# Gating two token tiles at once in an attention, MoE and FFN kernel on one Trainium2 core

## Chip, cores and metric

The kernel runs on one core of one Trainium2 chip. Its time is device microseconds of one execution; the median of a few executions is compared. The core's engines are TensorE (PE), VectorE (DVE), ScalarE (ACT), GpSimd (POOL) and SyncE (SP), which issues most of the DMAs. Each works through its own instructions in order and waits on semaphores for the others.

## What is computed

Three layers, each feeding the next, in float32; the token count N is 4 x 576 = 2304:

```python
# attention: 4 batches, 8 heads, 576 positions, 64 wide; window 128, ALiBi bias
scores = scale * np.matmul(q, k.transpose(0, 1, 3, 2))
mask = (rel >= 0) & (rel < window)
scores = np.where(mask, scores + bias[None], -1000000000.0)
attn = np.exp(scores - np.max(scores, axis=-1, keepdims=True))
attn = attn / (np.sum(attn, axis=-1, keepdims=True) + 1e-09)
x = np.matmul(attn, v)                                  # then (N, 512)
# mixture of 8 experts, 512 -> 1024 -> 512, two per token
noisy_logits = x @ w_gate + np.log1p(np.exp(x @ w_noise)) * noise
top2 = np.argpartition(-noisy_logits, 2, axis=1)[:, :2]  # weights: softmax over the two
out[mask] += top2_w[mask, k, None] * (np.maximum(x[mask] @ w1[e], 0.0) @ w2[e])
# FFN 512 -> 2048 -> 512
h = out @ w_in
r = np.maximum(h, 0.0)
result = (r * r) @ w_out
```

## The kernel before

The 2304 tokens are 18 tiles of 128. Attention takes a tile in two halves of four heads each, so there are 36 steps v. The order of the instructions is the order in which the Python code issues them; there is no scheduler. The loop over v (near the end of the function) does in each pass: `s_step(v + 2)`, `t_step(v + 1)`, `pv_step(v)` and the norm of v, so three steps are in work at once. Between these stand slots: `at(v, slot, f, ...)` files a piece of other work under a step and a slot, and `run(v, slot)` issues it. Slots 0 to 3 come after each head's score operation within `s_step`, slot 4 after the transposes, slot 5 after the norm.

- `s_step`: 16 QK matmuls (L245) into a `psb` bank; per head one VectorE operation (L255) that adds the bias, writes `p` and accumulates the row's extreme into `mx`; then the exponentials on ScalarE (L262). A row of scores spans 192 keys. Where a batch begins, part of them lies before the batch: `parts(i)` then cuts the 128 rows into two halves with different first columns, GpSimd writes 0 to the masked part (L251), and VectorE and ScalarE work on each half by itself (two instructions a head instead of one). These are the tiles 0, 4, 5, 9, 13 and 14, so 12 steps.
- `t_step`: six transposes of `p` on TensorE (L273) into `psa`, and two copies to `pt` on ScalarE (L275).
- `pv_step`: PV (L297) into the other `psb` bank; the norm on VectorE: L308 (the first reader), L311, L314, which writes half of the rows `xi`. After the second half SP sends `xi` to DRAM (L320).

The gate of tile i runs in the slots of the steps after v = 2i + 1. `gate_t` transposes `xi` on TensorE (L327) and copies it to `xt` on ScalarE (L329). `gate_m` multiplies with the gate weights (L335), then exponential and logarithm on ScalarE (L339, L340). `gate_o` finds the top two on VectorE (L345 to L357; L355 writes the one-hot `oh`). `rank` counts, with a triangular matrix, which row of its expert each token gets (L365), and adds `oh` to the running counts `acc` (L366). `place` works out the position in the table of slots on VectorE (L373 to L396), and GpSimd scatters the token numbers into it with two indirect DMAs (L400), a small memset of `spacer` (L399) ahead of each.

The gate's TensorE results share one PSUM bank, `psc`; `psa` has three and `psb` two (`bank`, L69). In every fourth step GpSimd also prepares a block of expert weights: a cast (L114) and a subtraction (L116) of 128 x 1024 elements. At the end of the attention SP reads the first expert's part of the table (L466), GpSimd gathers its rows (L413, three indirect DMAs), `x_in` transposes them (L420), and the first expert's matmuls begin (L437). The rest of the kernel, the experts (L437, L687) and the FFN (L794, L827), isn't touched.

Of the kernel before, what the change touches and what calls it, by code (L numbers as in the profile page):

```python
# [46 lines left out]
def attn_moe_ffn(ctx: ExitStack, tc: tile.TileContext, qt, kt, vt, wgn, noise, w1, w2, w_in, w_out,  # L47
# [180 lines left out]
    def s_step(v, now):  # L228
# [94 lines left out]
    def gate_t(i):  # L323
# [4 lines left out]
        G["xt", i] = wk.tile([128, 4, 128], F32, name="xt", tag="xt", bufs=2)  # L328
        nc.scalar.activation(out=G["xt", i], in_=ps, func=AF.Copy)  # L329

    def gate_m(i):
        gp = bank("c")
        xt = G.pop(("xt", i))
        for c in range(4):
            nc.tensor.matmul(gp[:, 0:16], xt[:, c, :], wg_sb[:, c, :], start=(c == 0), stop=(c == 3))  # L335
        gs = wk.tile([128, 8, 8], F32, name="gs", tag="gs", bufs=3)
        G["gs", i] = gs
        G["gp", i] = gp
        nc.scalar.activation(out=gs[:, 0], in_=gp[:, 8:16], func=AF.Exp)  # L339
        nc.scalar.activation(out=gs[:, 1], in_=gs[:, 0], func=AF.Ln, bias=1.0)  # L340

    def gate_o(i, n):
        gs = G["gs", i]
        if n == 0:
            nc.vector.tensor_tensor(out=gs[:, 2], in0=gs[:, 1], in1=nz_sb[:, i, :], op=OP.mult)  # L345
        elif n == 1:
            nc.vector.tensor_tensor(out=gs[:, 2], in0=gs[:, 2], in1=G.pop(("gp", i))[:, 0:8], op=OP.add)
        elif n == 2:
            nc.vector.max(out=gs[:, 3], in_=gs[:, 2])
        elif n == 3:  # L350
            nc.vector.max_index(out=sel[:, i, :], in_max=gs[:, 3], in_values=gs[:, 2])
        elif n == 4:
            oh = wk.tile([128, 2, 8], BF16, name="oh", tag="oh", bufs=3)
            G["oh", i] = oh
            nc.vector.tensor_tensor(out=oh, in0=iota8[:, None, :].to_broadcast([128, 2, 8]),  # L355
                                    in1=sel[:, i, 0:2, None].to_broadcast([128, 2, 8]), op=OP.is_equal)
            nc.vector.tensor_tensor(out=gap[:, i:i + 1], in0=gs[:, 3, 1:2], in1=gs[:, 3, 0:1], op=OP.subtract)  # L357

    def rank(i):
        oh = G["oh", i]  # L360
        rk = bank("c")
        G["rk", i] = rk
        for m, (l, r) in enumerate(((tri, oh), (ones, acc))):
            for k in range(2):
                nc.tensor.matmul(rk[:, 0:8], l, r[:, k, :], start=(m + k == 0), stop=(m + k == 2))  # L365
        nc.vector.tensor_tensor(out=acc, in0=acc, in1=oh, op=OP.add)  # L366

    def place(i, n):
        gs, oh = G["gs", i], G["oh", i]
        t, pf = gs[:, 4], gs[:, 5, 0:2]  # L370
        if n == 0:
            G["ri", i] = wk.tile([128, 2, 8], I32, name="ri", tag="ri", bufs=2)
            nc.vector.tensor_copy(G["ri", i][:, 0], G.pop(("rk", i))[:, 0:8])  # L373
            return
        ri = G["ri", i]
        if n == 1:
            nc.vector.tensor_scalar(ri[:, 1], ri[:, 0], 7, None, op0=OP.logical_shift_right)
            nc.vector.scalar_tensor_tensor(out=t, in0=ri[:, 0], scalar=float(E * NJ), in1=base8, op0=OP.mult,
                                           op1=OP.add)
            if i == EARLY:  # L380
                nc.vector.tensor_copy(snap[:, 0, 0:1], ri[0:1, 0, 0:1])
            if i == FIRST:
# [504 lines left out]
```

## Time and profile before

| | us |
|---|---|
| three executions | 1077.39, 1080.24, 1073.08; median 1077.39 |
| the profiled execution | 1080.85, of which span 1079.1 |
| busy TensorE, VectorE, ScalarE, GpSimd | 1033.2, 531.6, 419.0, 190.6 |
| mean granted TensorE clock | 0.964 of full |

Times in the profile are microseconds. The granted clock is the share of full speed that TensorE is given; it has two levels, 1.2 and 2.4 GHz, so that a mean between 0.5 and 1 says how long it stood at each. A row of a timeline is the start, the length and a run of alike instructions; in brackets stands the idle time of that engine just before it, and which instruction's end released it.

### The profile page before, as it was taken

To read this page: it belongs to the slowest core of one execution; us is meant where nothing else is said; L and a number is where in the kernel's file an instruction comes from. 1 tells how busy PE (TensorE), PEld (TensorE's weight loads), DVE (VectorE), ACT (ScalarE), POOL (GpSimd) and SP (SyncE) were. 2 spreads that over 40 slices of the span, in tenths; PEclk is the share of its full clock that TensorE was granted. 3 is DMA by queue.
4 is the path that set the end of the run, shared out by engine and by line. 5 is a ranking of instruction groups with operands and counts; after the bars stand their busy time and mean duration, and the time that the engine had idled before them with its cause. 6 is when DMAs were issued, how large, how long until landed. Compare 5 with 4: busy or idle time off the path is not lost. (4 is left out here: it accounts for less than half of the span.)

```text
span 1079.1 us, 18812 instructions
## 1 busy us (share of the span) xinstructions
PE 1033.2 (96%) x7518; PEld 922.7 (86%) x7518; DVE 531.6 (49%) x1429; ACT 419.0 (39%) x799; POOL 190.6 (18%) x238
## 2 busy tenths in 40 slices
PE   7888887999999999999999999999999999999998
PEld 5666666988989898989898988998989989899897
DVE  4787774445757666675756234622414123141330
ACT  6766673333434334343433334522413223131321
POOL 2344442310302121121203000301001010000000
PEclk8898976899999999999999999999999999999999
DMA  8554441335564746464645326501011010100000
GB/s 305 198 183 160 163 148 51 104 103 176 181 219 157 221 155 219 167 224 146 225 166 196 108 71 215 177 21 49 30 40 33 27 50 20 49 21 20 11 11 20
DMA packets 53233, 130.53 MB, mean 121 GB/s; under 512 B 7168, under 2 KB 9488, under 8 KB 52752
## 3 DMA queue, kind: packets, MB, share of 16 engines
q1 hardware_dynamic: 45600, 108.22, 30.1%
q0 software_dynamic: 7536, 21.02, 6.2%
q8 instruction: 61, 1.00, 0.4%
q14 instruction: 36, 0.29, 0.1%
HBM read 99.81 MB, written 29.40 MB: 120 GB/s over the span
## 5 line engine op out<-in xcount | busy, mean ns | idle before, releaser
L794 PEld LDWEIGHTS psa<-xf,w 128*128 128x128 f32 x1728 | 207.1, 190 | 2.2 <-DVE xf L422 1.2
L794 PE MATMUL psa<-xf,w 128*128 128x256 f32 x1728 | 207.6, 282 | 1.0 <-DVE xf L422 1.0
L801 DVE TENSOR_TENSOR gt<-gr,psa 128x512 f32<-128x512 f32 x72 | 49.5, 687 | 215.1 <-ACT gr L800 214.9
L437 PE MATMUL psa<-xa,w 128*128 128x384 f32 x768 | 144.8, 338 | 0.0
L687 PE MATMUL psb<-w,ha 128*128 128x512 f32 x552 | 137.0, 397 | 0.0
L437 PEld LDWEIGHTS psa<-xa,w 128*128 128x128 f32 x768 | 133.2, 190 | 0.6
L116 DVE TENSOR_TENSOR w<-raw,w 128x1024 fp32r<-128x1024 f32 x68 | 83.8, 1232 | 80.4 <-ACT w L112 80.0
L687 PEld LDWEIGHTS psb<-w,ha 128*128 128x128 f32 x552 | 100.9, 188 | 20.1
L827 PE MATMUL psb<-w,g 128*128 128x512 f32 (+1 forms) x456 | 103.8, 380 | 0.0
L827 PE MATMUL psb<-wx,g 128*128 128x512 f32 (+1 forms) x456 | 103.5, 380 | 0.0
L437 PE MATMUL psa<-xb,w 128*128 128x256 f32 x768 | 100.9, 282 | 1.3 <-ACT xb L421 0.9
L437 PEld LDWEIGHTS psa<-xb,w 128*128 128x128 f32 x768 | 98.4, 189 | 1.6 <-ACT xb L421 1.0
L612 POOL DMA_INDIRECT yr<-yg,pos x36 | 35.7, 992 | 341.7 <-DVE yr L619 210.9
L827 PEld LDWEIGHTS psb<-wx,g 128*128 128x128 f32 x456 | 81.9, 188 | 15.4
L827 PEld LDWEIGHTS psb<-w,g 128*128 128x128 f32 x456 | 81.3, 188 | 15.1
L591 POOL TENSOR_TENSOR dcc<-dca,dcc 128x512 f32<-128x512 f32 x32 | 41.6, 1300 | 287.1 <-DVE dca L589 145.0
L687 PE MATMUL psb<-w,hb 128*128 128x512 f32 x384 | 92.1, 393 | 0.0
L112 ACT ACTIVATE w<-raw 128x1024 fp32r<-128x1024 f32 x68 | 71.9, 1057 | 41.8 <-DMA raw<-in_w_dram 26.9
L262 ACT ACTIVATE p<-p,mx 128x192 f32<-128x192 f32 (+3 forms) x192 | 75.5, 422 | 31.5 <-DVE mx L255 29.0
L800 ACT ACTIVATE gr<-psa 128x512 f32<-128x512 f32 x72 | 43.0, 598 | 114.9 <-PE psa L794 114.0
L687 PEld LDWEIGHTS psb<-w,hb 128*128 128x128 f32 x384 | 71.6, 188 | 15.3
L441 ACT ACTIVATE ha<-psa 128x384 fp32r<-128x384 f32 x64 | 31.5, 492 | 105.8 <-PE psa L437 102.2
(108 smaller groups left out, 1169.7 us busy)
## 6 DMA issues: line engine op xcount, KB each, us to landing
raw<-in_w_dram SPq DMA_DIRECT2D x64, 512.0 KB
v<-in_vt_dram SPq DMA_DIRECT2D x20, 520.0 KB
yg<-yo SPq DMA_DIRECT2D x40, 256.0 KB
bits<-in_w_in_dram SPq DMA_DIRECT2D x16, 512.0 KB
bits<-in_w_out_dram SPq DMA_DIRECT2D x16, 512.0 KB
xd<-xi SPq DMA_DIRECT2D x18, 256.0 KB
q<-in_qt_dram SPq DMA_DIRECT2D x17, 256.0 KB
out_dram<-yo SPq DMA_DIRECT2D x17, 256.0 KB
```

The lines of the kernel that those rows point to most:

```text
L112: nc.scalar.activation(out=c[:, 0, :], in_=r, func=AF.Copy)
L116: eng.tensor_tensor(out=c[:, 1, :], in0=r, in1=c[:, 0, :].bitcast(F32), op=OP.subtract)
L262: nc.scalar.activation(out=p2[j][p0:p1, a, c0:], in_=p2[j][p0:p1, a, c0:], func=AF.Exp, bias=mx[j][p0:p1, a:a + 1], scale=-1.0)
L437: nc.tensor.matmul(o, w[:, wp, f * 128:(f + 1) * 128], x[:, xp, d, :], start=(n == 0), stop=(n == 11))
L441: nc.scalar.activation(out=hi, in_=ps, func=AF.Relu)
L591: nc.gpsimd.tensor_tensor(out=cf, in0=af, in1=cf, op=OP.add)
L612: nc.gpsimd.indirect_dma_start(out=YR[i, k], out_offset=None, in_=yg, in_offset=bass.IndirectOffsetOnAxis(ap=pos[:, i, k:k + 1], axis=0))
L687: nc.tensor.matmul(py, h[:, hq], wc[:, wp, wsl], start=(f + n == 0), stop=(f == 7 and n == 2))
L794: nc.tensor.matmul(ph[:, f % 2, :], wc[:, wp, fs], xf[:, xp, d, 0:BLK], start=(n == 0), stop=(n == 11))
L800: nc.scalar.activation(out=gr, in_=ph, func=AF.Relu)
L801: nc.vector.tensor_tensor(out=gt, in0=gr, in1=ph, op=OP.mult)
L827: nc.tensor.matmul(py[:, c0:c1], g[:, f, gq, j * 128:(j + 1) * 128], wc[:, wp, w0 + c0:w0 + c1], start=(f + n == 0), stop=(f == 15 and n = ...
```

## The change

The gate works on pairs of tiles p, with v = 4p + 3 the pair's last step. The two transposes stay apart (steps 4p + 2 and 4p + 4, slot 4; `xt` gets four buffers), and the rest is issued once per pair: eight gate matmuls at step 4p + 5, slot 4; the VectorE operations on 2 x 8 columns at step 4p + 6, slots 0 to 2; the rank (12 matmuls, as the second tile of a pair also counts the first) at slot 5, behind PV; the positions at step 4p + 7, slots 0 to 3, with all four scatters at the last. Where a batch begins, the masked part is filled with 1e9 instead of 0, so that one exponential a head (scale -1) covers all 192 columns. The first expert's `x_in` and the readers of its first results move a slot or two.

```diff
-                    nc.gpsimd.memset(p2[j][p0:p1, :, 0:c0], 0.0)
+                    nc.gpsimd.memset(p2[j][p0:p1, :, 0:c0], 1.0e9)
...
-                for p0, p1, c0 in parts(i):
-                    nc.scalar.activation(out=p2[j][p0:p1, a, c0:], in_=p2[j][p0:p1, a, c0:], func=AF.Exp,
-                                         bias=mx[j][p0:p1, a:a + 1], scale=-1.0)
+                nc.scalar.activation(out=p2[j][:, a, :], in_=p2[j][:, a, :], func=AF.Exp, bias=mx[j][:, a:a + 1],
+                                     scale=-1.0)
...
+    def gate_m(p):
+        gp = bank("c")[:, 0:32].rearrange("p (q w) -> p q w", q=2)
+        for q in range(2):
+            xt = G.pop(("xt", 2 * p + q))
+            for c in range(4):
+                nc.tensor.matmul(gp[:, q, :], xt[:, c, :], wg_sb[:, c, :], start=(c == 0), stop=(c == 3))
...
+    def rank(p):
+        oh = G["oh", p]
+        rk = bank("c")[:, 0:16].rearrange("p (q w) -> p q w", q=2)
+        G["rk", p] = rk
+        for q in range(2):
+            terms = [(tri, oh[:, q])] + [(ones, oh[:, 0])] * q + [(ones, acc)]
+            for m, (l, r) in enumerate(terms):
+                for k in range(2):
+                    nc.tensor.matmul(rk[:, q, :], l, r[:, k, :], start=(m + k == 0),
+                                     stop=(m + k == len(terms)))
+        for q in range(2):
+            nc.vector.tensor_tensor(out=acc, in0=acc, in1=oh[:, q], op=OP.add)
...
+            for q in range(2):
+                for k in range(2):
+                    i = 2 * p + q
+                    nc.gpsimd.memset(spacer, 0.0)
+                    st = nc.gpsimd.indirect_dma_start(
...
-    for i in range(NT):
-        v = 2 * i + 1
-        at(v + 1, 4, gate_t, i)
-        at(v + 2, 0, gate_m, i)
-        for n, p in enumerate((3, 3, 4, 4, 5)):
-            at(v + 2, p, gate_o, i, n)
-        at(v + 3, 0, rank, i)
-        for n, p in enumerate((1, 2, 3, 4, 4, 5)):
-            at(v + 3, p, place, i, n)
+    last = NV - 1
+    for p in range(NT // 2):
+        v = 4 * p + 3
+        end = v == last
+        at(v - 1, 4, gate_t, 2 * p)
+        at(v + 1, 4, gate_t, 2 * p + 1)
+        at(v + 2, 0 if end else 4, gate_m, p)
+        o = v + 2 if end else v + 3
+        for n, c in enumerate((0, 0, 0, 1, 2)):
+            at(o, c, gate_o, p, n)
+        at(o, 5, rank, p)
+        for n, c in enumerate((0, 1, 1, 2, 2, 3)):
+            at(o + 1, c, place, p, n)
...
-    for j, p in enumerate(((-1, 4), (0, 0), (0, 4))):
+    for j, p in enumerate(((-1, 5), (0, 4), (0, 5))):
...
-    at(last + 2, 5, out_a, 0, 0)
+    at(last + 3, 4, out_a, 0, 0)
     at(last + 3, 4, mm1_a, 0, 2)
     at(last + 3, 5, out_a, 0, 1)
-    at(last + 4, 0, out_a, 0, 2)
+    at(last + 3, 5, out_a, 0, 2)
```

On TensorE, before, the steps around one tile's gate read like this (L365 rank, L327 gate transposes, L335 gate matmuls; L273, L297 and L245 are transposes, PV and QK):

```order
L365 LDWEIGHTS tri [waits DVE_49]
L365 MATMUL psc<-oh,tri 128x8 [waits Activation_49]
...
L365 LDWEIGHTS ones
...
L273 MATMUL psa<-cst,p_1887 128x128 [waits Activation_49] x2
...
L327 MATMUL psc<-cst,xi 128x128 [waits DVE_49]
L327 MATMUL psc<-cst,xi 128x128 x3
L297 MATMUL psb<-v,pt 64x65 [waits PE_49]
...
L245 MATMUL psb<-k,q 64x192 [waits DVE_49,PE_49]
...
L335 MATMUL psc<-wg_sb,xt 128x16 [waits Activation_49]
L335 MATMUL psc<-wg_sb,xt 128x16 x3
L273 MATMUL psa<-cst,p_1961 128x128 x3
...
L297 MATMUL psb<-v,pt 64x65 [waits DVE_49,PE_49]
```

After, the same engine from the gate matmuls of a pair (L336) to its rank (L371); L272, L296 and L245 are transposes, PV and QK, and L326 the gate transposes of the next pair's first tile:

```order
L336 MATMUL psc<-wg_sb,xt 128x16 [waits Activation_49]
L336 MATMUL psc<-wg_sb,xt 128x16 x7
L296 MATMUL psb<-v,pt 64x65 [waits DVE_49,PE_49]
...
L245 MATMUL psb<-k,q 64x192 [waits DMAHW2_49,DVE_49,PE_49]
...
L272 MATMUL psa<-cst,p_1756 128x128 [waits Activation_49] x2
...
L326 MATMUL psc<-cst,xi 128x128 [waits DVE_49,Activation_49]
L326 MATMUL psc<-cst,xi 128x128 x3
L296 MATMUL psb<-v,pt 64x65 [waits PE_49]
...
L371 LDWEIGHTS tri [waits DVE_49]
L371 MATMUL psc<-oh,tri 128x8 [waits Activation_49]
...
L371 LDWEIGHTS ones
```

The gate matmuls have moved from before the transposes of a step to behind them, and the rank from the head of a step to its end, behind the next pair's gate transposes and PV; it waits for VectorE and for ScalarE, as before.

On GpSimd, before, in a stretch of plain steps (L114 and L116 weights, L400 scatters):

```order
L114 CAST w_1726<-raw 128x1024 [waits DMAHW5_49,Pool_49]
L116 TENSOR_TENSOR w_1726<-raw,w_1726 128x1024 [waits Pool_49]
L399 MEMSET spacer 1x1
L400 DMA slots<-tok,pos 9728x1 [waits DMASW0_49,DVE_49]
L399 MEMSET spacer 1x1 [waits Pool_49]
L400 DMA slots<-tok,pos 9728x1 [waits DMASW1_49]
L399 MEMSET spacer 1x1 [waits Pool_49]
L400 DMA slots<-tok,pos 9728x1 [waits DMASW2_49,DVE_49]
```

After, at a burst that stands ahead of a batch's beginning (L413 scatters, L251 memset of the masked part):

```order
L412 MEMSET spacer 1x1
L413 DMA slots<-tok,pos 9728x1 [waits DMASW0_49,DVE_49]
L412 MEMSET spacer 1x1 [waits Pool_49]
L413 DMA slots<-tok,pos 9728x1
...
L413 DMA slots<-tok,pos 9728x1
L251 MEMSET p_780 64x2x64 [waits PE_49,Activation_49]
L251 MEMSET p_786 64x2x64 [waits PE_49,Activation_49]
...
L114 CAST w_987<-raw 128x1024 [waits DMAHW6_49]
L116 TENSOR_TENSOR w_987<-raw,w_987 128x1024 [waits Pool_49]
```

The scatters have moved together in fours, and the memset and the weight preparation of the steps that follow stand behind all four.

## Rows read from the trace of the kernel before

**Rows 1.** The page: the granted TensorE clock in 40 slices of 27 us.
```profile
PEclk8898976899999999999999999999999999999999
```

**Rows 2.** Windows of four steps: length, busy us (count) by engine, TensorE clock, DMA, GB/s.
```profile
48.40:67.84 19.44, 15.97 (x237) 12.67 (x232) 16.33 (x99) 16.04 (x42) 7.88 (x12) 0.90 0.49 165
67.84:86.37 18.53, 15.42 (x252) 11.77 (x248) 13.22 (x83) 10.57 (x31) 8.33 (x13) 0.91 0.51 179
...
148.01:169.16 21.15, 18.10 (x244) 14.58 (x239) 13.28 (x83) 12.30 (x34) 7.59 (x10) 0.74 0.35 114
169.16:195.82 26.66, 19.19 (x231) 16.35 (x223) 13.10 (x83) 9.12 (x23) 7.20 (x11) 0.63 0.20 60
```

**Rows 3.** Timeline of TensorE over one tile: start, us, instructions, idle before and releaser.
```profile
28.03 0.20 PE L365 MATMUL psc<-oh,tri 128*128 128x8 bf16 x2 [0.39 <-DVE oh L355]
...
28.14 0.85 PE L273 MATMUL psa<-cst,p 128*128 128x128 f32 x6
28.90 0.66 PE L327 MATMUL psc<-cst,xi 128*128 128x128 f32 x4
29.48 1.13 PE L297 MATMUL psb<-v,pt 128*64 128x65 f32 x32
30.43 0.83 PE L245 MATMUL psb<-k,q 64*64 64x192 f32 x16
31.33 1.06 PE L335 MATMUL psc<-wg_sb,xt 128*128 128x16 f32 x8
32.24 0.85 PE L273 MATMUL psa<-cst,p 128*128 128x128 f32 x6
```

**Rows 4.** Timeline of all engines at one weight preparation, 74.8 to 78.6 us.
```profile
74.89 1.04 POOL L114 CAST w<-raw 128x1024 fp32r<-128x1024 f32 x1
...
76.02 2.33 POOL L116 TENSOR_TENSOR w<-raw,w 128x1024 fp32r<-128x1024 f32 x1
...
76.46 1.93 DVE L355 TENSOR_TENSOR oh<-iota,sel 128x16 bf16<-128x16 uint32 x1
...
78.44 0.21 PE L365 MATMUL psc<-oh,tri 128*128 128x8 bf16 x2 [2.20 <-DVE oh L355]
```

**Rows 5.** Groups by line and shape, first 260 us: busy us, mean ns; idle before.
```profile
L355 DVE TENSOR_TENSOR oh<-iota,sel 128x16 bf16<-128x16 uint32 x18 | 11.2, 621 | 0.0
...
L366 DVE TENSOR_TENSOR acc<-acc,oh 128x16 bf16<-128x16 bf16 x18 | 6.0, 331 | 1.0 <-PE psc L365 0.8
```

**Rows 6.** Timeline of all engines in the tile of rows 3.
```profile
29.94 0.85 ACT L275 ACTIVATE pt<-psa 128x384 f32<-128x384 f32 x2
...
30.68 0.60 ACT L329 ACTIVATE xt<-psc 128x512 f32<-128x512 f32 x1
...
33.35 0.17 DVE L349 MAX8 gs<-gs 128x8 f32<-128x8 f32 x1
```

**Rows 7.** Timeline at two scatters (66 us) and at the early gathers (180 us).
```profile
66.09 0.99 POOL L400 DMA_INDIRECT slots<-tok,pos  x1 [0.22 <-issue]
...
67.84 0.16 DVE L308 TENSOR_SCALAR rs<-psb 128x4 f32<-128x4 f32 x1 [1.09 <-PE psb L297]
...
179.79 0.95 POOL L413 DMA_INDIRECT xr<-xd,gidx  x1 [0.30 <-issue]
...
181.94 0.16 DVE L308 TENSOR_SCALAR rs<-psb 128x4 f32<-128x4 f32 x1 [5.48 <-remote]
...
183.05 1.52 PE L273 MATMUL psa<-cst,p 128*128 128x128 f32 x6
```

**Rows 8.** The view of rows 5: exponentials, and the memset of the masked part.
```profile
L262 ACT ACTIVATE p<-p,mx 128x192 f32<-128x192 f32 x96 | 37.3, 445 | 19.0 <-DVE mx L255 19.0
...
L262 ACT ACTIVATE p<-p,mx 64x192 f32<-64x192 f32 x32 | 14.4, 451 | 5.2 <-DVE mx L255 4.3
...
L262 ACT ACTIVATE p<-p,mx 64x64 f32<-64x64 f32 x32 | 11.0, 345 | 6.1 <-DVE mx L255 5.3
...
L251 POOL MEMSET p<- 64x256 f32 x16 | 4.5, 319 | 0.2
```

More of the change, by code (lines that the diff above doesn't have):

```diff
@@ L327, in gate_t @@
             nc.tensor.transpose(ps[:, c, :], xi[:, c * 128:(c + 1) * 128], ident)
-        G["xt", i] = wk.tile([128, 4, 128], F32, name="xt", tag="xt", bufs=2)
+        G["xt", i] = wk.tile([128, 4, 128], F32, name="xt", tag="xt", bufs=4)
         nc.scalar.activation(out=G["xt", i], in_=ps, func=AF.Copy)
[L331 to L339, printed above, removed]
+    def gate_m(p):
[4 more added lines that the diff above has]
+                nc.tensor.matmul(gp[:, q, :], xt[:, c, :], wg_sb[:, c, :], start=(c == 0), stop=(c == 3))
+        gs = wk.tile([128, 8, 2, 8], F32, name="gs", tag="gs", bufs=2)
+        G["gs", p] = gs
+        G["gp", p] = gp
+        nc.scalar.activation(out=gs[:, 0], in_=gp[:, :, 8:16], func=AF.Exp)
@@ L340, in gate_m, with gate_o @@
         nc.scalar.activation(out=gs[:, 1], in_=gs[:, 0], func=AF.Ln, bias=1.0)
-    def gate_o(i, n):
-        gs = G["gs", i]
+    def gate_o(p, n):
+        gs = G["gs", p]
+        two = slice(2 * p, 2 * p + 2)
         if n == 0:
-            nc.vector.tensor_tensor(out=gs[:, 2], in0=gs[:, 1], in1=nz_sb[:, i, :], op=OP.mult)
+            nc.vector.tensor_tensor(out=gs[:, 2], in0=gs[:, 1], in1=nz_sb[:, two, :], op=OP.mult)
         elif n == 1:
-            nc.vector.tensor_tensor(out=gs[:, 2], in0=gs[:, 2], in1=G.pop(("gp", i))[:, 0:8], op=OP.add)
+            nc.vector.tensor_tensor(out=gs[:, 2], in0=gs[:, 2], in1=G.pop(("gp", p))[:, :, 0:8], op=OP.add)
@@ L354, in gate_o @@
[L354 to L366, printed above, removed]
@@ L368, in place @@
-    def place(i, n):
-        gs, oh = G["gs", i], G["oh", i]
-        t, pf = gs[:, 4], gs[:, 5, 0:2]
+            oh = wk.tile([128, 2, 2, 8], BF16, name="oh", tag="oh", bufs=2)
+            G["oh", p] = oh
+            nc.vector.tensor_tensor(out=oh, in0=iota8[:, None, None, :].to_broadcast([128, 2, 2, 8]),
+                                    in1=sel[:, two, 0:2, None].to_broadcast([128, 2, 2, 8]), op=OP.is_equal)
+            nc.vector.tensor_tensor(out=gap[:, two, None], in0=gs[:, 3, :, 1:2], in1=gs[:, 3, :, 0:1], op=OP.subtract)
@@ new lines, in rank @@
+    def rank(p):
[8 more added lines that the diff above has]
+                                     stop=(m + k == len(terms)))
+        for q in range(2):
+            nc.vector.tensor_tensor(out=acc, in0=acc, in1=oh[:, q], op=OP.add)
@@ L371, in place @@
+    def place(p, n):
+        gs, oh = G["gs", p], G["oh", p]
+        t, pf = gs[:, 4], gs[:, 5, :, 0:2]
         if n == 0:
-            G["ri", i] = wk.tile([128, 2, 8], I32, name="ri", tag="ri", bufs=2)
-            nc.vector.tensor_copy(G["ri", i][:, 0], G.pop(("rk", i))[:, 0:8])
+            G["ri", p] = wk.tile([128, 2, 2, 8], I32, name="ri", tag="ri", bufs=2)
+            nc.vector.tensor_copy(G["ri", p][:, 0], G.pop(("rk", p)))
             return
-        ri = G["ri", i]
+        ri = G["ri", p]
@@ L504, in attn_moe_ffn @@
     load_to(1)
-    for v in range(-2, NV + 4):
+    for v in range(-2, NV + 3):
         s_step(v + 2, v)
```

47 lines of the change are left out of this document (23 added, 24 removed).

## The prediction

> **What bounds the kernel now.** I read the page's slices first [rows 1]: the granted clock is below full in the first seven of 40 slices, some 190 us, which hold the attention with the gate. What follows is a matmul stream that the change doesn't touch, so only the first 200 us can move. Second I cut that stretch into windows of four half-tile steps, two token tiles each [rows 2]. The reader is to see that no engine is full: in 67.84 to 86.37 TensorE works 15.4 of 18.5 us, VectorE 13.2, ScalarE 10.6; in a window where a batch begins (48.40 to 67.84) VectorE and ScalarE come to 16. The stretch is a chain of hand-overs, and its last window, 26.66 us at a clock of 0.63, is the worst. Third, TensorE's timeline over a tile without trouble [rows 3]. From start to start: rank 0.11 us, transposes 0.76, gate transposes 0.58, PV 0.95, QK 0.90, gate matmuls 0.91. Four steps are 4 x (0.76 + 0.95 + 0.90) = 10.4 plus 2 x (0.11 + 0.58 + 0.91) = 3.2, so 13.6 us of work against 18.5. Two waits that the gate makes are in the same rows: 0.39 for `oh`, 0.41 for `xt`.
>
> **The change part by part.** The sum is made against the profiled execution's own 1080.85 us, which is 3.5 above the median of the runs shown (1077.39); the forecast is put on the median at the end.
>
> 1. *The collision.* VectorE's `oh` takes 1.93 us at 76.46, and ends within 0.05 us of GpSimd's weight subtraction (76.02 + 2.33); TensorE's rank waits 2.20 behind it [rows 4]. By line, L355 takes 621 ns on average over 18 and L366 331 ns, where a gate operation of this size takes 0.17 us alone [rows 5, 6]: 18 x (0.621 - 0.17) + 18 x (0.331 - 0.17) = 8.1 + 2.9 = 11 us, nearly all on TensorE's path. GpSimd works in order and runs ahead, so after the change its cast and subtraction, 3.5 us from 74.89 to 78.35, follow the burst of scatters of step 4p+3 (4.8 us, part 4), 8.3 us from that step's slot 3; the pair's gate operations come at step 4p+6, some 9 us after it by my schedule below. I take them as clear of each other, and the collision as gone: 1.9 us in a clean window. The margin is thin; without it rival 3 holds.
> The Trainium skill ("SBUF — State Buffer", Who interferes with whom) says that a VectorE operation with two SBUF inputs contends with a GpSimd instruction that reads SBUF, and that the loser is blocked for the whole of it. The trace agrees with that, by the 1.93 us above. By this rule the change only moves what is exposed, for most of the gate's operations have two SBUF inputs; that is rival 3 again, and with it the sum would come to about nothing.
>
> 2. *A new wait at the rank.* There is one `psc` bank. In step 4p+6 the rank comes behind PV, and between the gate matmuls and it lie the gate transposes of the next pair, so it starts only when ScalarE has copied those to `xt`. ScalarE, in order, comes to `xt` behind the step's exponentials and two `pt` copies [rows 6]. In the tile of before `xt` ended at 30.68 + 0.60 = 31.28, and PV's work at 30.43, where QK starts [rows 3]: 0.85 us late. To that comes VectorE: seven instructions of the pair's gate stand ahead of the step's first score operations, 0.17 us each [rows 6] and some 0.20 apart, which makes the exponentials, and so `xt`, 1.4 us later: 2.2 us. Bounds: 0 (ScalarE ahead) to 3.1 (one more `pt` copy in between); I take 2.2, which both rows give. Behind the waiting rank stand QK and the transposes, so all of TensorE stands.
>
> 3. *What goes with the pairing.* The waits of 0.39 and 0.41, twice a pair, go (1.6 us). Rank has 12 matmuls for two tiles, 0.33 us against 0.22. VectorE has some ten gate operations of 0.2 us fewer a pair, 2 us, hidden while VectorE works 13.2 of 18.5 us; were it the bound, they would be worth these 2 us. The gate matmuls are the same 1.8 us, in one place. By hand a pair is 13.7 of work, 2.2 at the rank and 1.1 for two QKs that wait for a last score operation: 17.0. The clock: after the long wait that ends at 181.94 six transposes take 1.52 us instead of 0.85 [rows 7, 3], and of a clean window I put 18.5 - 13.6 - 1.9 - 1.4 (small waits) = 1.6 down to it. Half of that, 0.8, I leave in, since a wait of 2 us remains: 17.8 against 18.5, so **-1.5** for the two clean windows. In 148.01 to 169.16, where the clock is 0.74 and the window 2.6 longer, I let two thirds of that stay and take the same 0.7: **-1.6**.
>
> 4. *One exponential a head where a batch begins.* A head costs 451 + 345 ns there against 445 for a whole one [rows 8]: 4 x 0.35 = 1.4 us less of ScalarE a step, 12 steps, worth something only where ScalarE ends last (16.04 of 19.44 us in the second window). Against it, the exponential now reads the masked part and so waits for GpSimd's memsets, 0.32 us each [rows 8], which stand behind four scatters of 0.99 with 0.22 between [rows 7]: 4.8 us. These begin at slot 3 of step 4p+7, the next step's exponentials about 3.0 later: a wait of 4.8 + 0.6 - 3.0 = 2.4, less the 1.4 saved, +1.0 where a beginning follows a burst. Of the four windows with a beginning one has no burst in the way (-0.7, half a step's saving), two have it fully (+1.0 each), one in part (+0.7): **+2.0**. Bounds: -5 (1.4 saved in about four steps, no wait) to +9 (2.4 in four, nothing saved).
>
> 5. *The tail.* After two scatters come three early gathers; L308 starts at 181.94, 1.2 us after the end of the last gather (179.79 + 0.95), having waited 5.48, and TensorE's rank waits behind the `oh` that follows it [rows 7]. After the change no gate operation stands behind that norm, so QK and transposes (0.90 + 0.76) run beside it. By hand: 13.5 of work (two QKs, four transposes, four PVs, the pair's gate, 12 transposes of gathered rows), 5.5 - 1.7 = 3.8 held, 1.8 for clock and small waits: 19.1 instead of 26.66, **-7.5**. Bounds: -2 (held in full, at half clock as now) to -9.5 (not held). The last burst comes a step later, and so do the table read on SP, the gathers behind it and the first expert's rows; one of its results is read a slot later: **+1.5** (0 to 4, what is covered by the last tiles' gate work and what isn't).
>
> Sum: -1.5 - 1.6 + 2.0 - 7.5 + 1.5 = -7.1; 1080.85 - 7.1 = 1073.7, and 3.5 lower on the median: **1070 us**.
>
> **The rivals.**
> *R1, slower: the burst holds TensorE.* L308 starts 0.76 us after a second scatter's end (66.09 + 0.99 to 67.84), having waited 1.09 us [rows 7]; the same stands at the gathers. If a norm can't start while such transfers are issued, four in a row hold it for 4.8 + 0.8 = 5.6 us from slot 3 of step 4p+7, of which 2.2 lie beside that step's work: 3.4 each. Four bursts in plain steps at 3.4, three others at 1.0 and four clock falls of 0.8 are +20: 1090. It decides from about 1.0 us a burst over seven bursts, where the gain of 7.1 is gone. For it: both rows, and that the hold grew from two transfers to five. Against it: a norm also waits for PV, whose end the rows don't show.
> The Trainium skill (same page and section) says that `tensor_scalar` can enter a mode that takes GpSimd's ports, and that the later of the two then blocks; L308 is a `tensor_scalar`. By it the price would be that of R1, and no run here shows yet which of them holds the norm.
> *R2, faster: no new wait.* If `xt` is early (the lower bound of part 2), 2.2 x 7 = 15.4 us go, and with no long wait the clock need not fall, 0.8 x 6 = 4.8: -20 from the forecast, 1050. For it: ScalarE works only 10.6 of 18.5 us. Against it: its order in [rows 6].
> *R3, the same: the collision moves.* If the cast and subtraction end later than I reckon, an operation of slot 0 is stretched as at 76.46, by 1.3 us in six pairs: +8, 1078. For it: a margin of 0.7 us. Against it: a shift of one queue by half a step makes it 2 us or none. Then the change does not take away the 11 us.
>
> **How the numbers follow.** Forecast, 1070 with an own range of 1060 to 1080: 0.40. R1, 1090: 0.22. R2, 1050: 0.25. R3, 1078: 0.13. A measurement of this kernel tells about 1% from no change: faster is below 1066.6, slower above 1088.2. Faster: 0.24 of R2 and 0.13 of the forecast, 0.37. Slower: 0.16 of R1 and 0.04 of the others, 0.20. Within 1%: the rest, 0.43. The range takes in R2 and most of R1: 1047 to 1092.
>
> **What would show it.** Right: `oh` and the add to `acc` near 0.17 us on average; the rank waiting some 2 us for ScalarE's `xt` in nearly every pair; a last window of 18 to 20 us. R1: the norm behind a burst starting 0.8 us after its last scatter, with TensorE idle for over 3 us in step 4p+7. R2: clean windows of 15 us and a clock near 1. R3: another gate operation at 1 us or more. Wrong altogether: time that moves behind 200 us, or windows with a beginning that lose more than 2 us each.

## The result and the profile after

| | before | changed |
|---|---|---|
| median of four executions, us | 1078.82 | 1089.09 |
| range, us | 1073.08 to 1080.24 | 1086.68 to 1090.26 |
| profiled execution, span, us | 1079.1 | 1086.4 |
| busy TensorE, VectorE, ScalarE, GpSimd, us | 1033.2, 531.6, 419.0, 190.6 | 1036.4, 507.0, 398.6, 190.1 |

The ratio is 1.0102, with a 95% interval of 1.0059 to 1.0146: the change makes the kernel 1% slower, where I had forecast 1070 and given slower by over 1% a chance of 0.20. VectorE and ScalarE each have over 20 us less to do, and it doesn't help.

The granted clock by slices shows where TensorE was throttled, as in [rows 1]:

```profile
PEclk9898869999999999999999999999999999999999
```

The last slice below 0.9 is the sixth, at some 160 us. In [rows 1] it is the eighth, at some 215 us; the prediction reads seven slices and 190 us there. The windows of four steps are cut at the norm of the same steps as in [rows 2], and the last ends with the first expert's first matmul (the first of the eight, from 23.41, is left out):

```profile
42.39:63.59 21.20, 17.40 (x226) 13.63 (x226) 12.96 (x88) 10.79 (x28) 8.27 (x14) 0.85 0.44 151
63.59:83.88 20.29, 16.19 (x250) 13.07 (x250) 10.02 (x74) 10.90 (x28) 7.61 (x10) 0.92 0.50 164
83.88:107.11 23.23, 18.65 (x226) 15.07 (x226) 11.94 (x90) 10.89 (x28) 9.38 (x18) 0.78 0.46 148
107.11:129.98 22.87, 19.40 (x250) 16.02 (x250) 10.13 (x74) 10.90 (x28) 7.61 (x10) 0.78 0.47 159
129.98:157.49 27.51, 21.01 (x238) 16.81 (x242) 15.98 (x106) 11.30 (x29) 9.21 (x18) 0.75 0.31 97
157.49:176.25 18.76, 15.73 (x242) 12.63 (x238) 10.01 (x71) 10.71 (x28) 7.60 (x10) 0.91 0.39 129
176.25:200.25 24.00, 17.30 (x228) 14.15 (x229) 10.40 (x64) 9.73 (x24) 8.23 (x14) 0.86 0.18 56
```

Against the windows of before (19.44, 18.53, 20.49, 18.73, 22.42, 21.15 and 26.66 us in the same order) the two plain ones, the second and the fourth here, are 1.8 and 4.1 longer, the three with a batch's beginning 1.8, 2.7 and 5.1 longer, and the last two 2.4 and 2.7 shorter. The start and the first window are 6.0 shorter, and what follows the last is 2.9 longer: together the 7.3 us between the spans. VectorE works 10.0 us in a plain window instead of 13.2, so it isn't work that is late.

By line the collision is gone, as counted on. These are the add to `acc` and the `oh` of the pair, in the first 260 us (busy us, mean ns), the answer to [rows 5]:

```profile
L374 DVE TENSOR_TENSOR acc<-acc,oh 128x16 bf16<-128x16 bf16 x18 | 3.0, 166 | 8.4 <-PE psc L371 8.1
...
L359 DVE TENSOR_TENSOR oh<-iota,sel 128x32 bf16<-128x32 uint32 x9 | 1.7, 190 | 0.1
```

Both are near 0.17 to 0.19 us, where they were 0.33 and 0.62. What took its place stands in the view of waits (total us, times, longest), first 215 us:

```profile
DVE rs L307 <- PE psb L296: 40.5, 21, 5.2
...
DVE rs L307 <- remote: 18.2, 5, 5.4
...
PE psc L371 <- ACT xt L328: 12.2, 7, 2.7
...
ACT p L261 <- POOL p L251: 11.1, 3, 4.7
```

The new wait at the rank is there, 1.7 us in each of seven pairs. So is a wait of the norm that is released by nothing the profile can name ("remote"; five of them, where the kernel before has the one of 5.48 in [rows 7]), and one of the exponentials for memsets. TensorE's timeline has the first of the three, the rank's wait, and below it the 16 gate matmuls of a pair, at half clock:

```profile
80.33 0.19 PE L371 MATMUL psc<-oh,tri 128*128 128x8 bf16 x2 [1.49 <-ACT xt L328]
...
92.66 3.59 PE L336 MATMUL psc<-wg_sb,xt 128*128 128x16 f32 x16
```

And this is one burst, at the end of step 4p + 7 in a plain stretch, all engines:

```profile
63.95 0.99 POOL L413 DMA_INDIRECT slots<-tok,pos  x1 [12.30 <-DVE rs L310]
...
65.25 0.99 POOL L413 DMA_INDIRECT slots<-tok,pos  x1 [0.21 <-issue]
...
65.76 1.29 PE L296 MATMUL psb<-v,pt 128*64 128x65 f32 x30
...
66.55 0.97 POOL L413 DMA_INDIRECT slots<-tok,pos  x1 [0.21 <-issue]
...
67.53 0.29 PE L296 MATMUL psb<-v,pt 64*64 64x65 f32 x2 [0.49 <-issue]
...
67.82 0.96 POOL L413 DMA_INDIRECT slots<-tok,pos  x1 [0.22 <-issue]
...
68.29 0.56 PE L245 MATMUL psb<-k,q 64*64 64x192 f32 x4 [0.47 <-issue]
...
69.73 1.57 PE L245 MATMUL psb<-k,q 64*64 64x192 f32 x12 [0.88 <-issue]
...
69.98 0.16 DVE L307 TENSOR_SCALAR rs<-psb 128x4 f32<-128x4 f32 x1 [3.38 <-remote]
...
71.23 1.54 PE L272 MATMUL psa<-cst,p 128*128 128x128 f32 x6
```

Four scatters run from 63.95 to 68.78. TensorE itself is broken into pieces: the last two matmuls of PV come after a gap of 0.49, and QK has gaps of 0.47 and 0.88, all of which wait for nothing shown. PV is through at 67.82, but the norm behind it starts only at 69.98, 1.20 after the last scatter; the next transposes start at 71.23 and run at half clock, 1.54 instead of 0.85. This is R1, and it is the same at each of the first seven bursts: no norm starts inside one, and the next starts 1.14 to 1.26 us after its end.

### The profile page after: what moved, and what is told of

The parts are those of the page before. It is cut to its first block, busy times and chain, and to the rows that moved or that the text cites. A ratio compares the mean times of both kernels' runs of the same rounds, so it can differ in the third digit from the quotient of the medians.

```text
span 1086.4 us, 18715 instructions
## 1 busy us (share of the span) xinstructions
PE 1036.4 (95%) x7536; PEld 926.4 (85%) x7536; DVE 507.0 (47%) x1330; ACT 398.6 (37%) x733; POOL 190.1 (18%) x238
## 3 DMA queue, kind: packets, MB, share of 16 engines
q1 hardware_dynamic: 45600, 108.22, 30.1%
## 5 line engine op out<-in xcount | busy, mean ns | idle before, releaser
L116 DVE TENSOR_TENSOR w<-raw,w 128x1024 fp32r<-128x1024 f32 x68 | 83.8, 1232 | 82.8 <-ACT w L112 79.5
L261 ACT ACTIVATE p<-p,mx 128x192 f32<-128x192 f32 x144 | 59.0, 449 | 83.2 <-DVE mx L255 66.6
L112 ACT ACTIVATE w<-raw 128x1024 fp32r<-128x1024 f32 x68 | 71.9, 1057 | 39.9 <-DMA raw<-in_w_dram 25.8
```

Of the source, the lines that this page charges most:

```text
L112: nc.scalar.activation(out=c[:, 0, :], in_=r, func=AF.Copy)
L116: eng.tensor_tensor(out=c[:, 1, :], in0=r, in1=c[:, 0, :].bitcast(F32), op=OP.subtract)
L261: nc.scalar.activation(out=p2[j][:, a, :], in_=p2[j][:, a, :], func=AF.Exp, bias=mx[j][:, a:a + 1], scale=-1.0)
```

## The experiments

The runs were made in five sets. A set runs on one chip, beside many executions of the kernel before on that chip, and its numbers are compared within it; the sets' chips differ, which turned out to matter. Where numbers of two sets are set against each other below, two chips are compared, and the difference is to be taken as rough. The ratio is an estimate from the executions and need not be the quotient of the two medians. For the long steps I add up, per run, the steps 8 to 35 (from norm to norm) by their place in a pair: A is 4p + 4, behind the burst, B the one with the gate matmuls, C the one with the rank, D the one with the positions. Each sum is of seven steps, from the starts of the norm's first operation in VectorE's timeline.

| run | set | A | B | C | D | median, us | ratio to before |
|---|---|---|---|---|---|---|---|
| before | result | 30.1 | 36.2 | 44.0 | 34.8 | 1078.82 | |
| changed | result | 44.5 | 46.5 | 28.2 | 37.6 | 1089.09 | 1.0102 (1.0059 to 1.0146) |
| n_before | 1 | 38.5 | 29.5 | 27.8 | 31.5 | 1056.54 | 0.9816 (0.9763 to 0.9870) |
| n_after | 1 | 24.8 | 31.6 | 24.9 | 45.4 | 1058.72 | 0.9844 (0.9790 to 0.9898) |
| split | 1 | 35.3 | 36.7 | 26.9 | 40.4 | 1068.99 | 0.9932 (0.9899 to 0.9964) |
| gt_late | 1 | 43.5 | 41.7 | 25.9 | 27.2 | 1070.48 | 0.9925 (0.9886 to 0.9963) |
| fill | 2 | 25.4 | 44.9 | 26.2 | 39.7 | 1068.97 | 0.9952 (0.9928 to 0.9975) |
| combo | 2 | 35.2 | 33.8 | 25.8 | 28.5 | 1050.73 | 0.9777 (0.9740 to 0.9815) |
| before_again | 4 | 31.5 | 30.3 | 43.6 | 33.8 | 1068.63 | |
| after_again | 4 | 23.9 | 45.1 | 27.4 | 41.0 | 1069.94 | 1.0013 (0.9983 to 1.0042) |
| old_exp_again | 4 | 24.8 | 40.1 | 27.5 | 39.2 | 1061.39 | 0.9937 (0.9911 to 0.9962) |
| combo_again | 4 | 24.9 | 33.1 | 24.8 | 31.1 | 1041.28 | 0.9768 (0.9729 to 0.9807) |
| after_mask | 5 | 24.8 | 33.7 | 25.2 | 42.5 | 1056.48 | 0.9876 (0.9826 to 0.9926) |
| combo_mask | 5 | 26.4 | 30.8 | 22.7 | 29.7 | 1039.66 | 0.9738 (0.9688 to 0.9789) |

(The median in the row of before_again is that of 19 executions of the kernel before in that set.) The table already says it: the change takes 16 us out of C, where the collision was, and puts 14 into A, 10 into B and 3 into D.

### First set: is it the burst or the rank's wait?

**n_after**, the scatters left out of the changed kernel:

```diff
-                    nc.gpsimd.memset(spacer, 0.0)
-                    st = nc.gpsimd.indirect_dma_start(
-                        out=slots, out_offset=bass.IndirectOffsetOnAxis(ap=pos[:, i, k:k + 1], axis=0),
...
```

> The changed kernel without its 36 scatters (L413 and the spacer memsets; the table of slots stays at its zeros, so all gathers fetch the same row; the positions are still worked out). Theory 1 (four scatters in a row hold TensorE and the norm behind them): the step after a burst falls from 6.3 us to about 3.6 and the clock falls that follow it go, over seven bursts 20 us or more: 1069 or less. Theory 2 (the rank's wait for xt, 1.5 us a pair, and the clock that falls after it): no more than 8 us are saved, 1081 or more.

**n_before**, the same lines left out of the kernel before.

> The kernel before without its 36 scatters (the same work left out). Theory 1: two in a row cost much less than four, so it saves 5 to 10 us, 1069 to 1074, clearly less than the same cut saves in the changed kernel. Theory 2: as much is saved here as there.

Before is at 1077.19 in this set. Without scatters the changed kernel is at 1058.7 and the one before at 1056.5: 0.9844 and 0.9816 of before, against 1.0102 (in the result) and 1. Theory 1 holds in its main point. The scatters cost the changed kernel 2.6% and the one before 1.8%, and A falls from 44.5 to 24.8. But theory 1 had no room for the rest: it allowed the kernel before 5 to 10 us, and 20.7 came, and with no scatter at all the pairing gains nothing either. D is 45.4 there. A part of that is GpSimd's weight subtraction, which with no burst ahead of it runs earlier and meets position operations: four of them take 0.84 to 1.92 us, 4.7 us more in all than alone. One of the four, and two of the lines (mean ns, first 200 us; 173 and 172 in the changed kernel):

```profile
133.70 2.35 POOL L116 TENSOR_TENSOR w<-raw,w 128x1024 fp32r<-128x1024 f32 x1
...
134.16 1.92 DVE L385 TENSOR_SCALAR ri<-ri 128x16 int32<-128x16 int32 x1
...
L385 DVE TENSOR_SCALAR ri<-ri 128x16 int32<-128x16 int32 x9 | 3.5, 387 | 0.1
...
L397 DVE TENSOR_TENSOR gs<-gs 128x16 f32<-128x16 f32 x9 | 3.0, 337 | 0.1
```

So the pairing doesn't remove the collision for good: without the burst, 4.7 of the 11 us that it cost before are back.

**split**, the second tile's position and scatters one step later:

```diff
+        at(o + 1 if end or p == 6 else o + 2, 3, place, p, 6)
```

> The changed kernel with the second tile's position and its two scatters one step later (the pairs of tiles 12, 13 and 16, 17 stay as they are). Theory 1: two holds of some 0.8 us replace one of 3 in six pairs, and fewer clock falls: 1070 to 1080. Theory 2: within 4 us of the changed kernel.

**gt_late**, the first tile's gate transposes behind the rank:

```diff
-        at(v - 1, 4, gate_t, 2 * p)
+        at(v - 1 if end else v, 4, gate_t, 2 * p)
```

> The changed kernel with the gate transposes of a pair's first tile one step later, behind the rank of the pair before, so that the rank no longer waits for ScalarE's copy. Theory 1: at most 1.5 us in seven pairs are saved, 1078 to 1086, and the steps after the bursts stay at 6.3 us. Theory 2: with the wait the clock falls go too: 1070 or less.

Both are better than the changed kernel's ratio in the result by 1.7 to 1.8%. For split that is what theory 1 said, and 1 us more: A falls by 9, B by 10. For gt_late theory 2 is right: D falls by 10.4 and B by 4.8, and the granted clock from 27 to 200 us is 0.89 instead of 0.83, while A stays at 43.5, as theory 1 had it. Neither theory alone has both; there are two costs.

### Second set: what holds the norm?

**b_burst**, the kernel before with an even tile's scatters issued with the odd tile's:

```diff
-            for k in range(2):
...
+            for m in (i - 1, i) if i % 2 else ():
+                for k in range(2):
```

> The kernel before with one edit: the two scatters of an even tile are issued only with those of the odd tile after it, four in a row. Theory 1 (four in a row hold TensorE and the norm): about 2.5 us and a clock fall more in seven places, 1077 becomes 1090 to 1100. Theory 2 (the cost of a scatter is the same wherever it stands, and the change is slow by its rank wait): within 5 us of 1077.

Measured: 1070.84, a ratio of 0.9950 (0.9928 to 0.9973) to 1075.02. Neither theory said faster, and the trace shows that the run isn't the test it was meant to be. The first two of the four no longer wait for anything new when GpSimd comes to them, so they run at once, still in twos. What changed is where the weight preparation falls: `oh` takes 277 ns on average over 18 instead of 621 [rows 5],

```profile
L355 DVE TENSOR_TENSOR oh<-iota,sel 128x16 bf16<-128x16 uint32 x18 | 5.0, 277 | 0.0
```

and C falls from 44 to 29 us. But A rises from 30 to 40, and other gate operations are stretched in place of `oh`, among them this one, which takes 0.17 us alone:

```profile
70.26 1.89 DVE L377 TENSOR_SCALAR ri<-ri 128x8 int32<-128x8 int32 x1
```

It says nothing on bursts, and once more that the collision hangs on GpSimd's order.

**fill**, each scatter replaced by GpSimd work without a DMA:

```diff
+                    nc.gpsimd.tensor_copy(fill[:, 0:2], pos[:, i, k:k + 1].to_broadcast([128, 2]))
+                    nc.gpsimd.memset(fill, 0.0)
+                    nc.gpsimd.memset(fill, 0.0)
```

> The changed kernel with each scatter replaced by GpSimd work of about its length (a two-column copy that reads the position, two memsets of 128 x 352; the table stays at its zeros, as without the scatters). If GpSimd's being busy is what holds the others (a port, or the queue of memsets and weight preparation behind it), the time stays at 1080 to 1090 and the norm after a burst still starts late. If the issuing of indirect DMAs is, it is 1056 to 1066, as without the scatters, and the norm starts with the end of PV.

1068.97, between the two answers, and the step sums say why: A is 25.4, as without scatters, B is 44.9, as with them. The norm no longer waits for GpSimd. Here it starts when PV is through, inside the row of fills:

```profile
64.95 1.13 PE L297 MATMUL psb<-v,pt 128*64 128x65 f32 x32
...
65.93 0.39 POOL L416 MEMSET fill<- 128x352 f32 x1
66.14 0.16 DVE L308 TENSOR_SCALAR rs<-psb 128x4 f32<-128x4 f32 x1 [1.00 <-PE psb L297]
...
66.63 0.39 POOL L415 MEMSET fill<- 128x352 f32 x1
```

So the hold in A is from the indirect DMAs, their issue or their transfers, and not from GpSimd being busy. And roughly 0.011 of the 0.026 that the scatters cost (0.9952 and 1.0102 against 0.9844, from three sets) come from its being busy: what stands in its queue behind the burst is late. That shows in B, 44.9 here and 31.6 without the work.

**l307_tt**, the norm's first operation as a tensor_tensor:

```diff
-            nc.vector.tensor_scalar(G["rs", i, g][:, 0], px[:, :, :, 64:65], 1e-9, None, op0=OP.add)
+            nc.vector.tensor_tensor(out=G["rs", i, g][:, 0], in0=px[:, :, :, 64:65], in1=tiny, op=OP.add)
```

> The changed kernel with the norm's first operation (L307, a tensor_scalar that adds 1e-9) written as a tensor_tensor with a tile of 1e-9. If VectorE's tensor_scalar is blocked by GpSimd's port while the scatters are issued, the norm no longer waits for the burst's end: 1070 to 1078, and TensorE has no gaps in the burst. If TensorE itself is held there, the same wait stands in the new operation: 1085 to 1092.

1090.43, ratio 1.0123 (1.0078 to 1.0168): nothing changes. The new operation waits in the same way, 1.1 us past the end of the last scatter at 72.02:

```profile
71.05 0.97 POOL L415 DMA_INDIRECT slots<-tok,pos  x1 [0.23 <-issue]
...
73.13 0.16 DVE L309 TENSOR_TENSOR rs<-psb,tiny 128x4 f32<-128x4 f32 x1 [3.32 <-remote]
```

The rule of the Trainium skill that I had set beside R1 ("SBUF — State Buffer", Who interferes with whom: `tensor_scalar` can enter a mode that takes GpSimd's ports, if its operands meet that mode's conditions) is therefore not what holds the norm here. The gaps inside PV and QK say that TensorE's side is held as well.

**combo**, split and gt_late together.

> The changed kernel with both earlier edits, the later gate transposes and the second tile's scatters a step later. If the rank's wait and the burst are two separate costs, 1053 to 1060; if each edit only avoids the same clock falls, 1064 to 1070, no better than one of them alone.

1050.73, 0.9777 of before, a little under the range for two separate costs: they add up, nearly in full (3.3% together, 1.7 and 1.8 apart). This version beats both kernels.

### Third set: the exponentials and the small transfers

**old_exp**, the changed kernel with two exponentials a head and 0 in the masked part:

```diff
-                    nc.gpsimd.memset(p2[j][p0:p1, :, 0:c0], 1.0e9)
+                    nc.gpsimd.memset(p2[j][p0:p1, :, 0:c0], 0.0)
...
-                nc.scalar.activation(out=p2[j][:, a, :], in_=p2[j][:, a, :], func=AF.Exp, bias=mx[j][:, a:a + 1],
...
+                for p0, p1, c0 in parts(i):
+                    nc.scalar.activation(out=p2[j][p0:p1, a, c0:], in_=p2[j][p0:p1, a, c0:], func=AF.Exp,
```

**b_exp**, the kernel before with the same lines the other way round.

> The changed kernel with the exponentials of before where a batch begins: 0 in the masked part, two exponentials a head. If the exponentials' wait for memsets that stand behind the burst outweighs the work saved, as I forecast (+2.0), it gets faster, 1084 to 1088; if the saved ScalarE work counts, slower, 1092 to 1098; if neither, within 2 us of 1089.

> The kernel before with that part of the change alone: 1e9 in the masked part, one exponential a head. Without bursts the memsets come early, so nothing waits and 1.4 us of ScalarE a step are saved in 12 steps: 1065 to 1072 if ScalarE is late there in most of them; 1075 to 1079 if something else is.

**sp_small**, each scatter replaced by a plain transfer from SP:

```diff
+                    nc.sync.dma_start(out=aside[i, :, k:k + 1], in_=pos[:, i, k:k + 1])
```

> The changed kernel with each scatter replaced by a plain transfer of the 128 positions to DRAM issued by SP (the table stays at its zeros). If the small transfers as such hold TensorE, the time stays above 1075 and the norm behind them is late; if it is GpSimd's issuing of indirect DMAs, 1056 to 1064, as without the scatters.

**singles**, combo with the scatters one at a time:

```diff
+        for n, (e, c) in enumerate(((2, 1), (3, 0), (3, 3)) if not end and p != 6 else ((1, 3),) * 3):
+            at(o + e, c, place, p, 6 + n)
```

> The kernel with the later gate transposes and its four scatters one at a time, each behind its own position operation: one at step 4p + 7 and three over the two steps behind it. If each issue costs TensorE the same, it stays at 1048 to 1055; if a single one is hidden and only a row of them holds, 1040 to 1046.

Before is at 1068.47 here, 7 to 9 us less than in the first two sets. old_exp came out at 1061.53, 0.9910 (0.9874 to 0.9947), 28 us under the changed kernel, which fits none of the three answers; b_exp at 1064.76, 0.9973 (0.9945 to 1.0001); sp_small at 1074.32, 1.0058 (1.0034 to 1.0082); singles at 1052.17, 0.9834 (0.9802 to 0.9866). The traces told what was odd. In old_exp a norm starts in the midst of each of the first eight bursts, and A is 25.7 us there and 24.0 in singles. The hold wasn't there on this chip. So sp_small says nothing on the hold, singles is no better than combo where there is none (0.9834 against 0.9768 in the next set), and old_exp couldn't be compared with the changed kernel of another set. b_exp, within the set, shows that one exponential a head is worth 0 to 0.6% by itself.

### Fourth set: the same kernels on one chip

> The changed kernel once more, unaltered, beside the three below. If the wait of the norm for the end of the scatters belongs to the kernel, ratio 1.010 to before and the norm never starts inside a scatter. If it belongs to the chip that a run fell on (it isn't in the profiles of the four kernels of the third set, where before is at 1068), a run on a chip without it shows norms inside scatters, steps after a burst of 3 to 4 us, and a ratio of 0.990 to 1.000.

> The kernel before once more, for its profile on the same chip. If the wait belongs to the chip, its norms also start inside scatters where the changed kernel's do, and not where they don't.

> The changed kernel with the two exponentials a head of before, beside the changed kernel itself. If that edit is what made it 1061, it is 20 us or more under it here too; if the chip was, the two are within 5 us of each other.

> Later gate transposes and the second tile's scatters a step later, once more. If both edits hold wherever it runs, ratio 0.975 to 0.985 to before; if the scatters' part only counts on a chip that shows the wait, nearer to the later transposes alone, 0.985 to 0.995.

The set decides. The unaltered changed kernel is at 1069.94 here, 1.0013 of before, and A is 23.9 us where it was 44.5. The kernel before is faster too, and its norms start 0.04 to 0.55 us after the end of eight of its pairs of scatters, where in the first profile they start 0.73 to 0.89 after nine of them. The hold belongs to the chip, or to something that stays with it for a set; the result and sets 1 and 2 have it, sets 3 to 5 don't. It isn't without exception where it is: in split (82.66) and combo (97.27) a norm starts 0.04 and 0.08 us into a later scatter of a row.

One thing more sets the two kinds of set apart. The profiles of before, changed, split, gt_late, l307_tt and combo give no landing time for any of their DMAs, that of b_burst for 15 of 29 rows, those of sets 3 to 5 that have scatters for 26 or more. The same row for the changed kernel and for after_again (KB, us to landing):

```profile
xd<-xi SPq DMA_DIRECT2D x18, 256.0 KB
...
xd<-xi SPq DMA_DIRECT2D x18, 256.0 KB, 2.2
```

So the recording differed too, and whether it has a part in the hold was not tested.

old_exp_again is 8.5 us under after_again, not 20 and not within 5: part of that edit is real. combo has the same ratio on both kinds of chip, 0.977, though its A is 35 on one and 25 on the other. The kernel before is longer on the first kind as well (its 28 steps take 145.1 us in the result and 139.2 in set 4), which accounts for a part of that.

What is left of the loss on a chip without the hold is in B, 45.1 against 30.3, and 12.0 of these 14.8 us are in three steps, 9, 17 and 25: 7.8, 10.9 and 9.5 us against 5.5, 5.1 and 5.6 before. These are the ones where a batch begins behind a burst. Step 17 of after_again, all engines:

```profile
84.86 0.96 POOL L413 DMA_INDIRECT slots<-tok,pos  x1 [0.21 <-issue]
...
85.27 0.16 DVE L307 TENSOR_SCALAR rs<-psb 128x4 f32<-128x4 f32 x1
...
86.13 0.96 POOL L413 DMA_INDIRECT slots<-tok,pos  x1 [0.21 <-issue]
...
87.09 1.97 POOL L251 MEMSET p<- 64x256 f32 x8
...
87.95 1.49 ACT L261 ACTIVATE p<-p,mx 128x192 f32<-128x192 f32 x4 [4.76 <-POOL p L251]
...
88.45 1.04 PE L272 MATMUL psa<-cst,p 128*128 128x128 f32 x3 [2.50 <-ACT p L261]
...
90.73 3.60 PE L336 MATMUL psc<-wg_sb,xt 128*128 128x16 f32 x16
...
96.21 0.16 DVE L307 TENSOR_SCALAR rs<-psb 128x4 f32<-128x4 f32 x1 [7.83 <-PE psb L296]
```

The norm at 85.27 starts inside a scatter, so nothing holds it. But eight memsets of the masked part, for two steps, stand behind the burst and start at 87.09. The exponentials wait 4.76 us for the first of them and the transposes 2.50 for the exponentials. TensorE then falls to half clock, just when the pair's 16 gate matmuls come, 3.60 us instead of 1.8, and the norm of the step waits 7.83.

The exponentials' reading of the masked part is not the whole of it. In old_exp_again they don't read it, and B is still 40.1, steps 9 and 17 still 8.3 and 9.3 us. The transposes read the masked part in every version, the kernel before included, and in step 17 of old_exp_again they wait for the same memsets behind the burst:

```profile
87.05 1.35 PE L273 MATMUL psa<-cst,p 128*128 128x128 f32 x6 [2.15 <-POOL p L251]
```

### Fifth set: the memsets away from the burst

```diff
-                    nc.gpsimd.memset(p2[j][p0:p1, :, 0:c0], 1.0e9)
+                    nc.vector.memset(p2[j][p0:p1, :, 0:c0], 1.0e9)
```

> The changed kernel with the memset of the masked part on VectorE instead of GpSimd, so that it no longer stands behind the burst. If the memsets behind the burst are what makes the steps with a batch's beginning long (steps 9, 17 and 25 took 7.8, 10.9 and 9.5 us in the repeat), these fall to 5 or 6 us and the ratio to before falls by about 0.010 against the changed kernel's on a chip of the same kind: 0.990 without the hold of the norm, 1.000 with it. If VectorE's own load takes it back, within 0.003.

> The kernel with later transposes and split scatters, with the same edit. Its exponentials wait for the memsets 5.7 us in all: 2 to 5 us under it, ratio 0.972 to 0.975, if that is on the path; 0.977 or more if VectorE pays for it.

after_mask is at 0.9876 of before (0.9826 to 0.9926) where after_again, on another chip without the hold, was at 1.0013 (0.9983 to 1.0042): 14 thousandths, or 15 us, a little more than expected. B falls from 45.1 to 33.7, steps 9, 17 and 25 to 4.8, 7.2 and 4.8. The same place:

```profile
80.05 0.92 DVE L251 MEMSET p<- 64x256 f32 x4
...
83.00 0.96 POOL L413 DMA_INDIRECT slots<-tok,pos  x1 [0.22 <-issue]
...
83.27 0.16 DVE L307 TENSOR_SCALAR rs<-psb 128x4 f32<-128x4 f32 x1
...
83.89 0.88 PE L272 MATMUL psa<-cst,p 128*128 128x128 f32 x6
```

VectorE writes the four masked parts in 0.92 us before the scores, and the transposes no longer wait. combo_mask, 0.9738, is the fastest kernel of the study; by the median it is 1.6 us better than combo_again, though the intervals of the two ratios overlap, so that its gain over combo isn't established. Three of its windows, one without a batch's beginning, one with it, and the last:

```profile
59.03:73.18 14.15, 13.75 (x250) 11.20 (x251) 9.92 (x73) 10.73 (x29) 7.59 (x10) 1.00 0.78 251
73.18:88.52 15.34, 13.69 (x226) 10.97 (x226) 13.63 (x96) 11.43 (x28) 7.57 (x10) 1.00 0.55 179
...
136.68:155.24 18.56, 15.24 (x228) 12.34 (x228) 10.16 (x64) 10.19 (x26) 9.28 (x15) 0.91 0.24 74
```

A plain window is 14.15 us at full clock, 13.75 of it TensorE at work: nearly the 13.6 us of work that I had counted for one, with the waits gone.

## Why the prediction was wrong

Two steps failed. The sum put the wait of the norm behind a burst at nothing, though R1 had a price for it; it measured 2.9 us in each of seven pairs on the chip of the result. And the term for the beginnings of batches, +2.0, measured +7.2. By the profiles the forecast was off by 14.4 us (+7.3 where -7.1 was forecast). The same two kernels differ by -4.9 in set 4, so that 12.2 of the 14.4 lie between the two kinds of set (one profile of each; by the medians, 1.0102 against 1.0013, it is some 9 us), where the hold is the difference that the traces show.

**Part 1, the collision: right in size, by luck of the queue.** `oh` and the add are at 0.17 to 0.19 us, and C, seven steps, falls by 15.8 us on the chip of the result and 16.2 in set 4, 2.3 a pair where I took 1.9 for a clean window. But R3's mechanism is real: n_after shows the subtraction meeting position operations when no burst is ahead of it, 1.92 us for L385 at 134.16, and 387 ns and 337 ns by line instead of 0.17 us. The Trainium skill ("SBUF — State Buffer", Who interferes with whom) names both of these forms as exposed, a `tensor_scalar` (L385), if its operands meet the mode's conditions, and an operation with two SBUF inputs (L397), and the trace agrees.

**Part 2, the rank's wait: right.** It is 12.2 us in seven pairs, so 1.7 each where 2.2 was forecast. gt_late takes 10.4 from D.

**Part 3, the plain windows: wrong on this chip.** -1.5 was forecast and it is +5.9 (20.29 and 22.87 against 18.53 and 18.73). In set 4, where nothing holds the norm, the same two are 16.87 and 16.81 against 19.04 and 17.61, -3.0. The difference is R1. I put it at 3.4 us for a plain burst; seven A steps took 44.5 us with the hold and 23.9 without it, 2.9 each, 20.6 in all, and R1's time of 1090 is what was measured. That the total fits so well is partly luck, since R1 left the misses of parts 4 and 5 and the gain at the start out. But the mechanism stood in the text near the right price, and the mistake is the chance of 0.22 and a sum that took none of it: the rows at 66.09 and 181.94 [rows 7] showed the norm waiting past the end of two scatters and of five transfers, and I took the longer hold as needing more evidence, not the shorter as a lower bound. What I held against R1, that PV's end isn't in the rows, stood in the same trace:

```profile
66.82 0.28 PE L297 MATMUL psb<-v,pt 64*64 64x65 f32 x5
```

PV's last matmuls end at 67.10 and the norm starts at 67.84, 0.74 later, where at 63.62, with no scatter, it follows PV by 0.06. That another chip does without the hold could not be read from one trace. The window of part 3 with the low clock, -1.6 by forecast, gave -2.4 here and -6.4 in set 4, where its clock is 1.00 instead of 0.65.

**Part 4, where a batch begins: the term that was mis-sized.** +2.0 was forecast. The four windows give -2.4, +1.8, +2.7 and +5.1, +7.2 in all, and in set 4 -2.5, +2.5, +2.9 and +4.4, +7.3, with no hold at all. The step that failed is "a wait of 4.8 + 0.6 - 3.0 = 2.4, less the 1.4 saved". The transposes' wait was 2.50, near enough, behind one of 4.76 for the exponentials; but the saving counts for nothing behind such a wait, the norm and the PV behind it wait too, and the clock falls exactly ahead of the gate matmuls that the change has gathered into one piece. after_mask, which takes only the memset off that queue, gives back 14 thousandths; putting the two exponentials back gives 8.5 us, as the transposes still wait for the memsets. My upper bound of +9 held, and my sign for being wrong altogether came, in the windows of +2.7 and +5.1.

**Part 5, the tail: too much.** -7.5 was forecast, -2.7 came (24.00 against 26.66). In set 4 the window is 19.17, my 19.1, but there before has 21.98, so the gain is 2.8. The 5.48 us that I subtracted from was again the hold, which the changed kernel keeps (5.37 at its gathers). Of the later burst +1.5 was forecast; what follows the last window is 2.9 longer (2.2 in set 4), since the first expert's second part waits 1.66 us for its rows, which come later, instead of 0.93, and goes on at a lower clock (0.93 from 225 to 250 us). The start, which I left out, gained 3.6; 1.6 of it lies ahead of the first norm, where no gate work stands in either kernel, and 2.0 behind it, in steps that have no gate work now.

Taken together, in set 4 the profiled executions give 1065.8 against 1070.7, -4.9, near the forecast's -7.1; but that is luck, as parts 4 and 5 miss by 5.3 and 4.7 us, and the window of the low clock gives 4.8 more than forecast and the start 2.2. By the medians it is no change, 1.0013. The forecast was for a chip without the hold, and I had before me the trace of one with it.

## What to carry to other kernels

When small operations are gathered into one burst, look at the queue that the burst stands in: here four scatters in a row made what came behind them on GpSimd late, memsets that the exponentials waited up to 4.8 us for, and taking those off the queue was worth some 15 us, twice what the change was meant to bring. A wait that a trace shows at a small burst was here a lower bound for the larger one (0.7 to 0.9 us past two scatters, 1.1 to 1.3 past four), not a curiosity, and the end of the work ahead of it, which decides whether it is a wait, stood in the same trace. And an edit that adds a dependency (a full-width exponential on the masked part) should be priced in the place with the longest queue, with the clock fall that follows the wait.

## What was not expected of the hardware

While GpSimd issued indirect DMAs, the norm on some chips started, with few exceptions, only 0.7 to 1.3 us after the last of them, and PV and QK had gaps of up to 0.88 us; on others it started in their midst. The chip, or what stays with it for a set, made 6 to 10 us of difference to the kernel before (1077.19 and 1075.02 against 1068.47, 1068.63 and 1067.11) and 19 to the changed one (1089.09 against 1069.94); how much of it is the hold was not separated. The hold needs the indirect transfers and not GpSimd's work (fill), and it isn't a matter of the waiting instruction's form (l307_tt). What it is was not found: whether plain small transfers would do the same could not be seen, since sp_small fell on a chip without it, and neither the chip nor the recording was varied by itself.
